# Two score banks as one PSUM tile or as two, the maxima taken apart by head, and another order of the program

## The chip, the core and the metric

The kernel runs on one core of a Trainium2 chip. The metric is device time in microseconds (us). TensorE is called PE below, VectorE DVE, ScalarE ACT, GpSimd POOL; SP issues the DMAs.

## The reference

Attention over 4 batches and 8 heads (576 positions, head size 64, keys masked by blocks of 64), and behind it two MLP layers on the 2304 rows of width 512:

```python
scores = scale * np.matmul(q, k.transpose(0, 1, 3, 2))
scores = np.where(block_i >= block_j, scores, -1000000000.0)
scores = scores - np.max(scores, axis=-1, keepdims=True)
attn = np.exp(scores)
attn = attn / (np.sum(attn, axis=-1, keepdims=True) + 1e-09)
x = np.matmul(attn, v)                     # rows: batch, position; columns: head, 64
...
h = x @ w_in                               # layer 1: 512 to 2048
g = h * np.tanh(np.where(h > 20.0, h, np.log1p(np.exp(np.minimum(h, 20.0)))))
x = g @ w_out                              # 2048 to 512
...
h = np.maximum(x @ w_in2, 0.0)             # layer 2
out = h * h @ w_out2
```

The MLP weights come as float64. The kernel decodes them to fp32 on DVE and ACT.

## The kernel before

**Chunks and passes.** The rows are cut into six chunks of 384 (`CH1`). Chunks 0 and 1 hold the first 192 positions of the batches (`attention_lo`, in fp32), chunks 2 to 5 the other 384 positions of one batch each (`attention_hi`, 4 head pairs a chunk, so 16 pairs). Each chunk goes through both MLP layers, a pass for each, in the order of `PASSES`. A pass is 16 steps of 128 hidden columns: 12 matmuls into `hp` (L1209), the activation `h` on ACT (L1215), the split of g into two fp16 halves (L1034 on ACT or L1035 on POOL, then L745 on DVE), and 12 matmuls into the four accumulators `acc` (L1275). Products are made of three fp16 products, of high and low halves. These are the bulk of PE's work. The pass of chunk 0 in layer 1 is done in fp32 (L1229, L1244) while the weights are still being split (`decode`, `weigh`, `split`).

**A head pair in `attention_hi`.** A small matmul with a matrix of ones gives the scale of q and k over the partitions (L808, read by DVE at L811), another that of v (L760, L762). The scores of both heads go to two PSUM banks, head 0 to bank 0 and head 1 to bank 1 (L833; the mask is L836). DVE takes the maxima of both heads in one reduction (`peak`, L843). In the first of the three score tiles of a pair it also copies 128 further columns of each head out (L889), the tail of the third tile. `low` scales the maxima (L846), ACT takes exp with a running sum, once for each head (`expo`, L851). `finish` normalizes and splits (L870 on ACT, L745 on DVE) and issues the transposing DMA (L874). Four head pairs later the product with v follows (L931), into bank 0, and ACT takes it out (L944).

**The two banks.** Both are one PSUM tile, `spare`, [128, 2, 512]. Columns 0 to 447 of each bank hold scores, the product with v, or a work tile of `attention_lo`. The last 64 columns of bank 0 hold the small sums: of q and k (`qm`), of v (`vm`), of the weights (`sc`, L1081, read by DVE at L1087) and of a chunk's maxima (`sx`, L1151, read at L1153). The other six banks are the four `acc` and the two `hp`.

**What sets the order.** Every step is a task with an engine, its reads and its writes. A planner (`Sched`) once put them in order with assumed durations; the result is stored as a string (`PLAN`), which `planned` decodes: the place of each task, and its engine where there is a choice. Each engine runs its part of this list strictly in order. The planner keeps engines off a bank by `opened`: PE waits for the last ACT or DVE access of the bank, ACT and DVE for the last of PE. The waits in the program itself are put in by the tile framework, from the accesses in the order of the list. `norm` adds the squares of a chunk on ACT (L1168) and DVE (L1171, L1172) and sums them on PE into `hp` (L1173).

Of the kernel before, what the change touches and what calls it, by code (L numbers as in the profile page):

```python
# [58 lines left out]
def seg_len(tiles):  # L59
# [35 lines left out]
    "RbG<*e9F+nSge_OR{Eg95a}g{kabXd%1P}m$F#rXlWzQeTwayYa<?4T2k_!S-K@i;JF8FXQ0XGiN*S|`+kUIPWPq&I&a#D@|5^UQ`F&-huFw&Z%;&H4Ik{B^"
    "OEX!`{2*y153zbB^QqcYzUHYf_N*;mXdh1d8vA76*A_CARm-%MRFmEMIjfdvN2w~G=}~sx$GvJHd7+kJ-+VOqNcTud`G8fO<wjP$r#H$w`U$$ct#`^oErnec"
    "=uGsP&-0u5KGF2Pu0*R<GFOYrySjoq&Cvn+sm{iJb99l`lf~Lr{z??)GYfUG<dFH2!_3tW**O)z&(l}6i8PS&+T7HW7c?r3&3Ua$)YX(pdaGQ~*Y&hKrN?!O"
    "rV?kb=qvK1p2Jr!==G9Be5Gmwd4?GIiw@J0#Me-r!0N&Jy6lqT=BT#OW^%pMVyv{;gO_&d24eew?vRINootgXx=p_$vQzW{?$8f!7L@OGl=Rl`i2Qs~PTFc7"
    ">8@M#7H-{He$X%EGi-d9b|Al&={jt`o_M;Q+oefCcC5v^Dda^LS*5w9slF*+YBOyl(}-px%e5Xm*UJ=HV4g$ACHjPXsMWNFwwB5A3bqw(&iinpuAE%P4~_6_"
    "C!+2jW+h(ei&w|W*YcLO<Fwaxo=!F&=~9`?$?tI99QJi2R_1798Dk!n8Js`bOw$?qju~YV_}ou=%XD383dvhiMFyKFJ9lB@J~G9O*YdJeCV&H*Ipq%NDql!h"  # L100
    "8AD{3#O`;=Nba1f<IDw_NE|$+BZ<Gf@|YRRX|36pQ$}ll{SRW|oU|~liLjAG)<n~s7#yKprH%~3Ly6K*?v%Goec7y!^8O%rGQ#xIfqEPGG#pFZB)!P+szg?2"
    "Jpd9kl?pNo1Zgbg&3#$~e|04KnqYxHYhSYaHqC1qf_4d<&`ArM=d_d7W^XT|sJ-Sfjr6kSk`6@KFL?D<ZKdVpJ!z%4W8+HP@DlU4Ni(vcJh50p8tcRQ2B_DF"
# [1496 lines left out]
```

## Time and profile before

| | before |
|---|---|
| median of 3 runs | 942.67 us (934.58 to 943.70) |
| profiled execution | 941.45 us, span 939.4 us |
| PE busy | 901.2 us, 96% of the span |
| ACT busy | 618.9 us, 66% |
| DVE busy | 574.7 us, 61% |
| mean granted clock of PE | 0.994 |

The span runs from the first to the last instruction of the profiled execution. A busy time is the time in which at least one instruction of the engine's datapath runs. The names in the rows are those of the program, without buffer numbers; `spare` is the tile of the two score banks, `pad` holds the results of exp, `late` and `pt` the transposed ones. A share over the span mixes stages, so the stretches matter more than the shares.

### The profile page before, as it was taken

What the parts mean: (1) busy time and instruction counts of PE and PEld (TensorE: products, weight loads), DVE (VectorE), ACT (ScalarE), POOL (GpSimd) and SP (SyncE); (2) the same over time, 40 slices, a digit from 0 to 9 for tenths busy, and PEclk for the clock granted to TensorE, in tenths of its full rate; (3) what the DMA queues carried; (4) which work ended last, traced back from release to release, by engine and by line L of the source; (5) the groups of instructions that cost most, each with busy time, mean ns of one, the idle gap of its engine ahead of it and who ended that gap; (6) DMA issues with size and microseconds to landing.
All of it is one profiled execution on the core that took longest, in us unless ns stands there. A gap on an engine that the chain in (4) does not pass through costs nothing. (4 is left out here: it accounts for less than half of the span.)

```text
span 939.4 us, 15711 instructions
## 1 busy us (share of the span) xinstructions
PE 901.2 (96%) x5786; PEld 532.3 (57%) x5786; DVE 574.7 (61%) x1386; ACT 618.9 (66%) x1177; POOL 82.5 (9%) x114
## 2 busy tenths in 40 slices
PE   7989997999999999999999999999999999999997
PEld 6655553555555555555556555555566666666664
DVE  6969998999989854455871486777441251331211
ACT  7979998998798875475892586676642242444442
POOL 0000101220110100011110011121100000000000
PEclk9999998999999999999999999999999999999999
DMA  9866576799668687786773378688832222333530
GB/s 350 293 223 235 206 184 191 183 289 290 245 216 234 199 226 228 193 169 229 195 153 99 113 204 226 164 201 178 199 102 68 68 68 68 112 135 135 168 112 34
DMA packets 141772, 168.79 MB, mean 180 GB/s; under 512 B 105856, under 2 KB 110976, under 8 KB 137600
## 3 DMA queue, kind: packets, MB, share of 16 engines
q1 hardware_dynamic: 141696, 167.80, 60.6%
q8 instruction: 45, 0.74, 0.3%
q14 instruction: 31, 0.25, 0.1%
HBM read 125.30 MB, written 17.30 MB: 152 GB/s over the span
## 5 line engine op out<-in xcount | busy, mean ns | idle before, releaser
L745 DVE SCALAR_TENSOR_TENSOR g<-h,cst,g 128x384 f16<-128x384 f32 x176 | 108.0, 617 | 233.5 <-ACT g L1034 222.7
L1215 ACT ACTIVATE h<-hp,cst 128x384 f32<-128x384 f32 x176 | 101.1, 577 | 216.4 <-PE hp L1209 211.1
L1275 PE MATMUL acc<-g,ws 128*128 128x384 f16 x1128 | 229.7, 326 | 2.7 <-DMA ws<-wspill 1.6
L1275 PE MATMUL acc<-g,raw 128*128 128x384 f16 x984 | 204.6, 326 | 0.0
L1209 PE MATMUL hp<-x,first 128*128 128x384 f16 x768 | 157.8, 330 | 3.8 <-ACT h L1215 3.8
L1275 PEld LDWEIGHTS <-ws 128*128 128x128 f16 x1128 | 108.7, 98 | 78.1 <-issue 5.4
L1209 PEld LDWEIGHTS <-first 128*128 128x128 f16 x960 | 92.7, 99 | 70.7 <-issue 13.0
L1275 PEld LDWEIGHTS <-raw 128*128 128x128 f16 x984 | 95.5, 98 | 63.0 <-issue 0.6
L1209 PE MATMUL hp<-x,raw 128*128 128x384 f16 x552 | 117.9, 326 | 0.0
L1209 PE MATMUL hp<-x,ws 128*128 128x384 f16 x408 | 85.0, 328 | 0.0
L1209 PEld LDWEIGHTS <-raw 128*128 128x128 f16 x648 | 61.6, 98 | 41.1 <-issue 2.0
L745 DVE SCALAR_TENSOR_TENSOR pb<-pad,st,pb 128x384 f16<-128x384 f32 (+2 forms) x96 | 72.0, 756 | 20.2 <-ACT pb L870 20.1
L1034 ACT ACTIVATE g<-h,cst 128x384 f16<-128x384 f32 x123 | 75.1, 612 | 13.3 <-PE acc L1275 12.5
L870 ACT ACTIVATE pb<-pad,st 128x384 f16<-128x384 f32 (+2 forms) x96 | 66.7, 711 | 15.0 <-DVE st L863 4.9
L851 ACT ACTIVATE pad<-spare,st,sq 128x448 f32<-128x448 f32 (+1 forms) x96 | 65.2, 680 | 15.8 <-DVE st L846 9.2
L1035 POOL TENSOR_SCALAR g<-h,cst 128x384 f16<-128x384 f32 x53 | 43.1, 815 | 342.5 <-PE acc L1275 129.7
L1209 PEld LDWEIGHTS <-ws 128*128 128x128 f16 x504 | 48.5, 98 | 32.3 <-issue 1.8
L843 DVE TENSOR_REDUCE st<-spare 128x2 f32<-128x896 f32 (+1 forms) x48 | 47.8, 996 | 11.4 <-PE spare L836 9.5
L1229 PE MATMUL hp<-xs,first 128*128 128x384 f32 x128 | 49.5, 495 | 0.1
L1220 ACT ACTIVATE h<-h 128x384 f32<-128x384 f32 x85 | 43.5, 513 | 0.8
L1209 PE MATMUL hp<-late,first 128*128 128x384 f16 x192 | 41.7, 326 | 0.0
L833 PE MATMUL spare<-q 64*128 64x448 f16 (+2 forms) x384 | 39.0, 309 | 2.7 <-ACT pad L851 1.6
(229 smaller groups left out, 1152.0 us busy)
## 6 DMA issues: line engine op xcount, KB each, us to landing
ws<-wspill SPq DMA_DIRECT2D x68, 512.0 KB, 4.4
...
```

The source lines that it names most:

```text
L745: return sch.add("DVE", c_dve(n) + 62 * ap, lambda: nc.vector.scalar_tensor_tensor(dst(), a(), s() if ap else s, c(), op0, op1), r=r, w=w, ...
L833: nc.tensor.matmul(out=pp.t[:, hd, o:o + k1 - k0], lhsT=qh.t[rows, u, a:a + 128], rhs=qh.t[rows, w, nq + k0:nq + k1], start=p == 0, stop=p ...
L843: sch.add("DVE", c_dve(2 * (o1 - o0)), lambda: nc.vector.reduce_max(both(st, j, r0), pp.t[r0:, :, o0:o1], axis=AX.X), w=[(pp, 0), (st, j)])
L851: t = sch.add("ACT", c_act(o1 - o0, True, 3), lambda hd=hd: nc.scalar.activation(pf[hd].t[r0:, k0:k0 + o1 - o0], pp.t[r0:, hd, o0:o1], AF. ...
L870: sch.add("ACT", c_act(n, False, 1), lambda pb=pb, pv=pv, s=s: nc.scalar.activation(pb.t[:, 0:i + 1, 0, :], pv(), AF.Copy, scale=s()), r=[ ...
L1034: "ACT": ("ACT", c_act(n, False, 1), lambda: nc.scalar.activation(dst(0), src(), AF.Copy, scale=s()), False),
L1035: "POOL": ("POOL", c_pool(n, False), lambda: nc.gpsimd.tensor_scalar(dst(0), src(), s(), 1.0, ALU.mult, ALU.mult), False),
L1209: nc.tensor.matmul(out=hp.t[:, 0:n], lhsT=w.t[:, f % 2, a, 128 * k:128 * k + 128], rhs=x.t[:, c, k, 0:n], start=k == 0 and i == 0, stop=k ...
L1215: sch.add("ACT", c_act(n, True, 1), lambda: nc.scalar.activation(h.t[:, 0:n], hp.t[:, 0:n], (AF.Mish, AF.Relu)[l], scale=hs()), r=[(cst, ( ...
L1220: "ACT": ("ACT", c_act(n), lambda: nc.scalar.activation(hv(), hv(), AF.Square), False),
L1229: nc.tensor.matmul(out=hp.t[:, 0:n], lhsT=wf.t[:, 512 * (f % 2) + 128 * k:512 * (f % 2) + 128 * k + 128], rhs=xs.t[:, k, 0:n], start=k == ...
L1275: nc.tensor.matmul(out=acc.t[:, 0:n], lhsT=wo.t[:, f % 2, a, 128 * m:128 * m + 128], rhs=g.t[:, c, 0:n], start=f == 0 and i == 0, stop=f = ...
```

## The change

The tile `spare` becomes two tiles of one bank each, `bank[0]` and `bank[1]`. The small sums move from bank 0 to the last 64 columns of bank 1. `peak` takes the maximum of each head by an instruction of its own, and the copy of the tail is two copies. The scores are declared by head, so that the exp of a head depends on its own bank; for the planner the product with v holds bank 0 alone, and `opened` now sets each of PE, ACT and DVE against both others. `PLAN` is another string of the same kind; it has 64 tasks more. Lines behind `low` stand 4 to 9 further down: L843 is L845, L851 is L856, L889 is L895, L1087 is L1096, L1172 is L1181, L1173 is L1182, L1209 is L1218, L1215 is L1224.

```diff
@@ -88,86 +88,87 @@
 PLAN = (
-    "c-p<13B1kay2qb)tz{l#i%q7=nDLlpR^&)U#xkXZGA5-==_t)nk{nVrA*ri_>f{iTkeSGAV{i7(W@Bggzt8>t|L=coyYBtmQ}>>8?bh1=^$ySbywC7^e$QS-"
...
+    "c-p<13B1ka_W#$j_ddo9A@dZ;JiBC`k|~sw5HgiAg=B~%6(Jdlx=K=plDhRvG)S7v5gCtpJjZxAhhzFa>;L{vn_K_a?{<Gv+y0)tpJ6@gS;J?2);UE)^;Rh<"
...
 )
@@ -278,7 +279,7 @@
 
     def opened(self, t, name):
 
-        others = ("ACT", "DVE") if name == "PE" else ("PE",)
+        others = [o for o in ("PE", "ACT", "DVE") if o != name]
         return max((self.shut[b, o] + self.SEM[o][name] for b in t.banks for o in others if (b, o) in self.shut), default=0.0)
 
     def fill(self, now, start, t):
@@ -681,13 +682,13 @@
     hps = [psp.tile([128, 512], F32, tag=f"hp{i}", name=f"hp{i}") for i in range(2)]
     R["hp"] = fixed(hps)
 
-    spare = {"ab": psp.tile([128, 2, 512], F32, tag="pab", name="spare")}
-    R["sc"] = fixed([spare["ab"][:, 0, 448 + 4 * i:452 + 4 * i] for i in range(4)])
-    R["qm"] = fixed([spare["ab"][:, 0, 464:472], spare["ab"][:, 0, 472:480]])
-    R["sx"] = fixed([spare["ab"][:, 0, 496:504], spare["ab"][:, 0, 504:512]])
-    R["vm"] = fixed([spare["ab"][:, 0, 480:488], spare["ab"][:, 0, 488:496]])
-    R["s1"] = fixed([spare["ab"][:, 1, 0:448], spare["ab"][:, 0, 0:448]])
-    R["ab"] = fixed([spare["ab"][:, :, 0:448]])
+    bank = [psp.tile([128, 512], F32, tag=f"bank{i}", name=f"bank{i}") for i in range(2)]
+    R["sc"] = fixed([bank[1][:, 448 + 4 * i:452 + 4 * i] for i in range(4)])
+    R["qm"] = fixed([bank[1][:, 464:472], bank[1][:, 472:480]])
+    R["sx"] = fixed([bank[1][:, 496:504], bank[1][:, 504:512]])
+    R["vm"] = fixed([bank[1][:, 480:488], bank[1][:, 488:496]])
+    R["s1"] = fixed([bank[1][:, 0:448], bank[0][:, 0:448]])
+    R["ab"] = fixed([[t[:, 0:448] for t in bank]])
     for key, extra in EXTRAP.items():
         R[key].bufs += extra
 
@@ -830,27 +831,31 @@
                 for p, (u, w) in enumerate(((0, 0), (1, 0), (0, 1))):
                     for hd in range(2):
                         rows = slice(64 * hd, 64 * hd + 64)
-                        nc.tensor.matmul(out=pp.t[:, hd, o:o + k1 - k0], lhsT=qh.t[rows, u, a:a + 128], rhs=qh.t[rows, w, nq + k0:nq + k1],
+                        nc.tensor.matmul(out=pp.t[hd][:, o:o + k1 - k0], lhsT=qh.t[rows, u, a:a + 128], rhs=qh.t[rows, w, nq + k0:nq + k1],
                                          start=p == 0, stop=p == 2 and not mask)
                 for hd in range(2 if mask else 0):
-                    nc.tensor.matmul(out=pp.t[:, hd, o + k1 - k0 - 64:o + k1 - k0], lhsT=above, rhs=never[:, 0:1].to_broadcast([128, 64]), start=False, stop=True)
-
-            steps.append(sch.add("PE", 3 * (c_mm16(k1 - k0) + 16) + (110.0 if mask else 0.0), mm, r=[(qh, (p, j)) for p in range(2) for j in range(2)], w=[(pp, 0)]))
+                    nc.tensor.matmul(out=pp.t[hd][:, o + k1 - k0 - 64:o + k1 - k0], lhsT=above, rhs=never[:, 0:1].to_broadcast([128, 64]), start=False, stop=True)
+
+            steps.append(sch.add("PE", 3 * (c_mm16(k1 - k0) + 16) + (110.0 if mask else 0.0), mm, r=[(qh, (p, j)) for p in range(2) for j in range(2)], w=[(pp, 0), (pp, 1)]))
 
         both = lambda st, j, r0=0: st.t[r0:, 2 * j:2 * j + 2]
 
-        def peak(st, j, pp, r0, o0, o1):
-            sch.add("DVE", c_dve(2 * (o1 - o0)), lambda: nc.vector.reduce_max(both(st, j, r0), pp.t[r0:, :, o0:o1], axis=AX.X), w=[(pp, 0), (st, j)])
-
-        def low(st):
+        def peak(st, j, pp, o0, o1):
+            for hd in range(2):
+                t = sch.add("DVE", c_dve(o1 - o0), lambda hd=hd: nc.vector.reduce_max(st.t[:, 2 * j + hd:2 * j + hd + 1], pp.t[hd][:, o0:o1], axis=AX.X),
+                            w=[(pp, hd), (st, (j, hd))])
+                t.banks = (hd,)
+
+        def low(st, r):
             sch.add("DVE", 69.0, lambda: nc.vector.tensor_scalar(both(st, 2), both(st, 0), sq.t[:, 5:6], None, ALU.mult),
-                    r=[(st, 0), (sq, 5)], w=[(st, 2)], lat=70.0)
+                    r=[(sq, 5), *r], w=[(st, 2)], lat=70.0)
 
         def expo(st, j, pp, r0, o0, o1, pf, k0):
+            view = lambda hd: pp.t[hd] if j == 4 else pp.t[:, hd]
             for hd in range(2):
                 t = sch.add("ACT", c_act(o1 - o0, True, 3), lambda hd=hd: nc.scalar.activation(
-                    pf[hd].t[r0:, k0:k0 + o1 - o0], pp.t[r0:, hd, o0:o1], AF.Exp, bias=st.t[r0:, 4 + hd:5 + hd], scale=sq.t[r0:, 4:5],
-                    accum_out=st.t[r0:, 2 * j + hd:2 * j + hd + 1]), r=[(st, 2), (sq, 4)], w=[(pp, 0), (st, (j, hd)), (pf[hd], k0)], table="exp")
+                    pf[hd].t[r0:, k0:k0 + o1 - o0], view(hd)[r0:, o0:o1], AF.Exp, bias=st.t[r0:, 4 + hd:5 + hd], scale=sq.t[r0:, 4:5],
+                    accum_out=st.t[r0:, 2 * j + hd:2 * j + hd + 1]), r=[(st, 2), (sq, 4)], w=[(pp, hd), (st, (j, hd)), (pf[hd], k0)], table="exp")
                 t.banks = (hd,) if j == 4 else ()
 
         def merge(st, j, op, r, w):
@@ -88,86 +88,87 @@
 PLAN = (
-    "c-p<13B1kay2qb)tz{l#i%q7=nDLlpR^&)U#xkXZGA5-==_t)nk{nVrA*ri_>f{iTkeSGAV{i7(W@Bggzt8>t|L=coyYBtmQ}>>8?bh1=^$ySbywC7^e$QS-"
...
+    "c-p<13B1ka_W#$j_ddo9A@dZ;JiBC`k|~sw5HgiAg=B~%6(Jdlx=K=plDhRvG)S7v5gCtpJjZxAhhzFa>;L{vn_K_a?{<Gv+y0)tpJ6@gS;J?2);UE)^;Rh<"
...
 )
@@ -911,12 +918,14 @@
                     qa = max(q0, 128 * c) - q0
                     for j, i in ((0, 0), (1, 0), (0, 1)):
                         for hd in range(2):
-                            streams[hd].append((ptv(hd)[:, 2 * c + i, qa:nq], av.t[64 * hd:64 * hd + 64, 0, qa:nq], part(j, c, hd)))
+                            streams[hd].append((ptv(hd)[:, 2 * c + i, qa:nq], av.t[0][64 * hd:64 * hd + 64, qa:nq], part(j, c, hd)))
                 products(streams)
 
             step = sch.add("PE", sum(3 * c_pair(nq - max(q0, 128 * c) + q0) for c in range(nch)) + 98, mm_av, r=[v3, *pts], w=[av])
             step.rows = 0.86
-            settle(lambda: av.t[:, 0, 0:nq], av, nq, x, hp, xo, sv)
+            settle(lambda: av.t[0][:, 0:nq], av, nq, x, hp, xo, sv)
+            for t in av.tasks:
+                t.banks = (0,)
             return [step]
 
         return steps, second
@@ -1493,12 +1502,12 @@
         for inst in R[key].insts:
             for t in inst.tasks:
                 if t.eng in ("PE", "ACT", "DVE") and t.banks is None:
-                    t.banks = (0, 1) if key == "ab" else (1 - inst.idx % 2,) if key == "s1" else (0,)
+                    t.banks = (0, 1) if key == "ab" else (1 - inst.idx % 2,) if key == "s1" else (1,)
...
```

The new order at three places. DVE, before, at the first score tile of head pair 2 in chunk 2: `st` are the maxima, `tl` the tail, `sq` the scale of the next pair, `nsq` the squares of a chunk, `wst` the sums of weights, `cst` and `x` the constants and halves of a chunk.

```order
L843 TENSOR_REDUCE st_1312<-spare 128x2
L1171 TENSOR_TENSOR nsq_1294<-nsq_1294,wsq_1307 128x768
L846 TENSOR_SCALAR st_1312<-st_1312,sq_1085 128x2
L745 SCALAR_TENSOR_TENSOR x_73<-xs_1149,cst_1215,x_73 128x384
L889 COPY tl_1327<-spare 128x256
```

And with the change:

```order
L1201 TENSOR_TENSOR cst_909<-cst_909 128x1
L746 SCALAR_TENSOR_TENSOR vs<-vs,sv_976 128x640
L845 TENSOR_REDUCE st_1318<-bank_133 128x1
L812 TENSOR_SCALAR sq_1286<-bank_134 128x2
L845 TENSOR_REDUCE st_1318<-bank_134 128x1
L813 TENSOR_SCALAR sq_1286<-sq_1286 128x2
L895 COPY tl_1333<-bank_133 128x128
L746 SCALAR_TENSOR_TENSOR x_73<-xs_1147,cst_1270,x_73 128x384
```

Each maximum and each tail copy is two instructions, with the scale of the next pair (L812, L813) between them.

DVE right behind that, before, to the step of the norm that PE's L1173 needs:

```order
L1195 TENSOR_TENSOR cst_893<-cst_893,wst_638 128x1
L811 TENSOR_SCALAR sq_1274<-spare 128x2
L745 SCALAR_TENSOR_TENSOR wn_66<-late,us_838,wn_66 128x1024
L745 SCALAR_TENSOR_TENSOR x_73<-xs_1149,cst_1215,x_73 128x384
L812 TENSOR_SCALAR sq_1274<-sq_1274 128x2
L1196 TENSOR_SCALAR cst_893<-cst_893 128x1
L1087 TENSOR_SCALAR wst_1071<-spare 128x2
L1172 TENSOR_TENSOR nsq_1294<-nsq_1294 128x384
L1029 TENSOR_SCALAR cst_893<-cst_893 128x1
```

With the change:

```order
L1204 TENSOR_TENSOR cst_909<-cst_909,wst_777 128x1
L814 TENSOR_SCALAR sq_1286<-sq_1286 128x2
L1180 TENSOR_TENSOR nsq_1326<-nsq_1326,wsq_1316 128x768
L1205 TENSOR_SCALAR cst_909<-cst_909 128x1
L895 COPY tl_1333<-bank_134 128x128
L1038 TENSOR_SCALAR cst_909<-cst_909 128x1
L850 TENSOR_SCALAR st_1318<-st_1318,sq_1041 128x2
L746 SCALAR_TENSOR_TENSOR wn_66<-late,us_829,wn_66 128x1024
L1181 TENSOR_TENSOR nsq_1326<-nsq_1326 128x384
L746 SCALAR_TENSOR_TENSOR pb<-pad,st_1128,pb 128x4x128
L746 SCALAR_TENSOR_TENSOR first<-first,us_453 128x1024
L1207 TENSOR_SCALAR cst_909<-wst_777,cst_909 128x16
```

The read of the weights' sum (L1087, now L1096) stood ahead of the norm's step L1172, now L1181; it has gone 24 rows behind it. A step of `finish` (`pb`) has come behind it instead.

ACT in chunk 2, later, at two exp groups of the next head pair: `h` is the activation of a pass, `ACT_TABLE_LOAD` the change between its table and that of exp.

```order
L851 ACT_TABLE_LOAD
L851 ACTIVATE pad,st_1753<-spare,st_1753,sq_1274 128x448
L870 ACTIVATE pb<-pad,st_1632 128x3x128
L851 ACTIVATE pad,st_1753<-spare,st_1753,sq_1274 128x448
L1215 ACT_TABLE_LOAD
L1215 ACTIVATE h_1811<-hp_131,cst_893 128x384
L1060 ACTIVATE wf<-raw_68 128x1024
L1078 ACTIVATE wsq_1848,us_1849<-wf 128x1024
L870 ACTIVATE pb<-pad,st_1632 128x3x128
L851 ACT_TABLE_LOAD
L851 ACTIVATE pad,st_1673<-tl_1651,st_1673,sq_1274 128x128
L851 ACTIVATE pad,st_1673<-spare,st_1673,sq_1274 128x448
```

With the change:

```order
L856 ACT_TABLE_LOAD
L856 ACTIVATE pad,st_1758<-bank_133,st_1758,sq_1286 128x448
L856 ACTIVATE pad,st_1758<-bank_134,st_1758,sq_1286 128x448
L1069 ACTIVATE wf<-raw_68 128x1024
L875 ACTIVATE pb<-pad,st_1625 128x3x128
L1087 ACTIVATE wsq_1846,us_1847<-wf 128x1024
L1043 ACTIVATE g_1858<-h_1782,cst_909 128x384
L875 ACTIVATE pb<-pad,st_1758 128x4x128
L1043 ACTIVATE g_1871<-h_1799,cst_909 128x384
L856 ACTIVATE pad,st_1745<-bank_133,st_1745,sq_1286 128x448
L856 ACTIVATE pad,st_1745<-tl_1639,st_1745,sq_1286 128x128
L856 ACTIVATE pad,st_1745<-bank_134,st_1745,sq_1286 128x448
```

The two exp of a tile follow each other, and the loads for one activation between this group and the next are gone.

## Rows read from the trace of the kernel before

**Rows 1.** The page: span; engine, busy us, share of the span, instructions.

```profile
span 939.4 us, 15711 instructions
...
PE 901.2 (96%) x5786; PEld 532.3 (57%) x5786; DVE 574.7 (61%) x1386; ACT 618.9 (66%) x1177; POOL 82.5 (9%) x114
```

**Rows 2.** Stretches: length, busy us (instructions) by engine, granted clock, DMA share, GB/s.

```profile
0.00:75.00 75.00, 64.73 (x336) 44.64 (x337) 58.79 (x160) 60.27 (x164) 1.05 (x10) 1.00 0.81 294
75.00:150.00 75.00, 72.99 (x322) 39.87 (x321) 73.46 (x177) 72.36 (x123) 7.33 (x10) 1.00 0.62 200
150.00:164.00 14.00, 9.47 (x51) 4.20 (x51) 10.15 (x31) 10.93 (x18) 1.70 (x3) 0.76 0.62 174
164.00:250.00 86.00, 79.24 (x565) 46.08 (x564) 83.32 (x175) 77.43 (x121) 13.67 (x15) 1.00 0.83 245
250.00:350.00 100.00, 94.91 (x628) 54.71 (x627) 80.61 (x202) 82.88 (x143) 12.78 (x16) 0.98 0.74 226
350.00:700.00 350.00, 345.47 (x2448) 201.85 (x2447) 208.81 (x523) 224.86 (x451) 41.99 (x54) 1.00 0.69 178
700.00:900.00 200.00, 200.00 (x1235) 120.41 (x1233) 52.74 (x114) 76.89 (x141) 4.00 (x6) 1.00 0.31 105
900.00:940.00 40.00, 34.43 (x212) 20.53 (x210) 6.80 (x11) 13.25 (x26) 0.00 (x0) 0.97 0.18 59
```

**Rows 3.** Waits of PE, 75 to 350: us, times, longest us.

```profile
PE hp L1209 <- ACT h L1215: 3.8, 4, 1.4
PE hp L1173 <- DVE cst L1029: 3.1, 1, 3.1
PE spare L1081 <- ACT pad L851: 1.8, 2, 1.0
PE acc L1275 <- DMA ws<-wspill: 1.6, 1, 1.6
PE spare L833 <- ACT pad L851: 1.6, 3, 1.0
```

**Rows 4.** Timeline of PE: start, us, line, operation, tiles, count, idle time before.

```profile
159.49 0.48 PE L1173 MATMUL hp<-nsq,ones 128*128 128x384 bf16 x1 [3.15 <-DVE cst L1029]
159.76 2.12 PE L1209 MATMUL hp<-x,first 128*128 128x384 f16 x6
...
163.03 1.14 PE L1209 MATMUL hp<-x,first 128*128 128x384 f16 x6
```

**Rows 5.** Timeline of DVE, around 159 us.

```profile
153.42 0.42 DVE L889 COPY tl<-spare 128x256 f32<-128x256 f32 x1
153.75 0.15 DVE L1195 TENSOR_TENSOR cst<-cst,wst 128x1 f32<-128x1 f32 x1
...
159.01 0.16 DVE L1087 TENSOR_SCALAR wst<-spare 128x2 uint32<-128x2 uint32 x1 [3.18 <-ACT pad L851]
159.09 0.35 DVE L1172 TENSOR_TENSOR nsq<-nsq 128x384 bf16<-128x384 bf16 x1
...
163.23 1.09 DVE L843 TENSOR_REDUCE st<-spare 128x2 f32<-128x896 f32 x1 [0.67 <-PE spare L836]
164.24 0.61 DVE L745 SCALAR_TENSOR_TENSOR g<-h,cst,g 128x384 f16<-128x384 f32 x1
```

**Rows 6.** Timeline of ACT, around 157 us.

```profile
156.97 1.28 ACT L851 ACT_TABLE_LOAD   x1
158.27 0.62 ACT L851 ACTIVATE pad<-spare,st,sq 128x320 f32<-128x320 f32 x1
```

**Rows 7.** Waits of DVE, 75 to 350, for exp.

```profile
DVE wst L1087 <- ACT pad L851: 9.9, 6, 3.2
```

**Rows 8.** Groups by line and shape: count, busy us, mean ns, idle before.

```profile
L843 DVE TENSOR_REDUCE st<-spare 128x2 f32<-128x896 f32 x32 | 34.7, 1084 | 5.9 <-PE spare L836 4.2 <-PE spare L833 1.8
...
L889 DVE COPY tl<-spare 128x256 f32<-128x256 f32 x16 | 6.6, 412 | 0.2 <-PE spare L1081 0.2
```

**Rows 9.** Stretch 75 to 350, DVE of line L843, then of L889.

```profile
75.00:350.00 275.00, 23.33 (x28) 0.98 0.73 222
...
75.00:350.00 275.00, 2.86 (x7) 0.98 0.73 222
```

**Rows 10.** Groups by line on ACT: table loads ahead of exp.

```profile
L851 ACT ACT_TABLE_LOAD x20 | 25.7, 1283 | 1.1 <-DVE us L1029 0.4 <-DVE cst L1183 0.3
```

More of the change, by code (lines that the diff above doesn't have):

```diff
@@ L95 @@
[L95 to L102, printed above, removed]
@@ L171 @@
+    "ga9pm@c8ORLv;3C7)<yf6q+g|?IEUzOfDz^5feJk1o!d`8$f3m-l27Ua^|}u78a$zkU@R~Mhrc8Q}P;#lfz)mjglRUGYAu}wh~g)pgshoGe`{yT9KO*%mj5W"
+    "q^dzj5%q~uG$^kgc1A<;8@s`QeHVM<0Z$Z(lb%@M{8-32V*!4|0&ED2ML_@m?6jyKF<#{{aRL|#1Ioj_ID-iqo#1NGfM^C~HAI*YD&y@#9Lr3cdc}ff<wm4L"
+    "ZUk4{Pf@?;xslB=Kfj`W5(b$haTtmC^fc<76rynGwy;JARUv5ALaF~_nD9R`92hNR7$Jn*yw3#4>)*nJ6-DB#E$SN~8n7b?b2}23E;lzyCXoGqc*}nQpW*$2"
+    "w$uylKi$xCwYhP{kSfLge91^)+nYe>FY5AtH4~4{_^b~ZvHyKd{y!7{@^jpo0sVG=Hxm1Q4mJu*"
 )
@@ L886, in attention_hi @@
                 steps.append(halves(vs, v3, sv, R["vm"].new()))
-            peak(st, 0, pp, 0, 0, n)
+            peak(st, 0, pp, 0, n)
             if i == 2:
-                sch.add("DVE", c_dve(256), lambda pp=pp, n=n: nc.vector.tensor_copy(tail.t, pp.t[:, :, n:n + 128]), w=[(pp, 0), tail])
-                peak(last, 1, tail, 0, 0, 128)
-            low(st)
+                for hd in range(2):
+                    t = sch.add("DVE", c_dve(128), lambda pp=pp, n=n, hd=hd: nc.vector.tensor_copy(tail.t[:, hd], pp.t[hd][:, n:n + 128]), w=[(pp, hd), (tail, hd)])
+                    t.banks = (hd,)
+                sch.add("DVE", c_dve(256), lambda: nc.vector.reduce_max(both(last, 1), tail.t, axis=AX.X), r=[(tail, 0), (tail, 1)], w=[(last, 1)])
+            low(st, [(st, (0, 0)), (st, (0, 1))])
             expo(st, 4, pp, 0, 0, n, pf, 0)
@@ L895, in attention_hi @@
         scores(4, pp, 0, 0, 448, False)
-        peak(last, 0, pp, 0, 0, 448)
-        merge(last, 0, ALU.max, [(last, 1)], [(last, 0)])
-        low(last)
+        peak(last, 0, pp, 0, 448)
+        merge(last, 0, ALU.max, [(last, 1), (last, (0, 0)), (last, (0, 1))], [(last, 0)])
+        low(last, [(last, 0)])
         expo(last, 5, tail, 0, 0, 128, pf, 448)
@@ L1500, in tile_attention_moe @@
             for _ in range(t.fillers or 0):
-                nc.tensor.matmul(out=spare["ab"][:, 1, 448:512], lhsT=ones, rhs=ones[:, 0:64], start=True, stop=True)
+                nc.tensor.matmul(out=bank[1][:, 448:480], lhsT=ones, rhs=ones[:, 0:32], start=True, stop=True)
             t.fn()
```

147 lines of the change are left out of this document (76 added, 71 removed).

## The prediction

> **What bounds the kernel now.** I read the page first: the span is 939.4 us and TensorE (PE) is busy in 901.2 of it [rows 1]. The change adds and removes no matmul, so all it can return or cost is PE's 38.2 us of idle time, and what PE loses at the lower clock. The view by stretches says where that is [rows 2]: 10.3 us before 75 us, 18.4 us from 75 to 350 us (2.0 + 4.5 + 6.8 + 5.1), 4.5 us from 350 to 700, nothing from 700 to 900, and 5.6 us at the tail, where the last output is written. The first two attention chunks, up to some 90 us, keep their order but for swaps of neighbours, and the tail is untouched. So the question is the 18.4 us from 75 to 350 us. There DVE is busy in 73.46 of 75 us, then in 83.32 of 86, and ACT in 72.36 of 75 and 77.43 of 86: PE is the bound, but two engines behind it have no slack, and what delays them reaches PE. After 350 us DVE is busy for 208.81 of 350 us, and small delays there are covered.
>
> The waits of PE in that stretch are many and small [rows 3]: 3.8 us for h (ACT's activation), 3.1 for one norm, 1.8 and 1.6 for an exp on the score banks, 1.6 for a DMA. The longest one shows a mechanism. The timeline of PE has the norm's matmul L1173 at 159.49, 3.15 us late [rows 4]. DVE stood idle for 3.18 us before L1087, the read of a small sum (two columns of bank 0), and the norm's own step L1172 is queued right behind it [rows 5]. L1087 waited for ACT's exp of head 0 on other columns of the same bank, which began only at 158.27, after a table load of 1.28 us [rows 6]; it ended at 158.89 and DVE went on at 159.01. So readers of one bank exclude each other here, though neither writes it, and the planner of before knew nothing of that (its rule for a bank sets ACT and DVE against PE alone). The cluster around it, 150 to 164 us, is dear: 4.5 us of PE idle, and a granted clock of 0.76 [rows 2]. That mean is 6.7 us at 1.2 GHz and the rest at 2.4, or some 3.4 us of work lost: six matmuls of L1209 take 2.12 us at 159.76 and 1.14 us at 163.03 [rows 4].
>
> **The change, part by part.** *Two tiles for one.* No instruction moves by that; which waits exist is settled by bank, as it was.
>
> *Maxima and tail copy by head.* 48 reductions become 96 and 16 copies 32: 64 more DVE instructions, with as many elements in all. The price of one is the fixed part. One bound is the duration: 1084 ns for 896 columns and 412 ns for 256 [rows 8] are 1.05 ns a column and 143 ns fixed. The other is the spacing of starts on a busy DVE: L889 to the next 0.33 us, L843 (896) to the next 1.01 us [rows 5], which is 1.06 ns a column and about 60 ns fixed, since an instruction starts before the last one's row ends. I take 66 ns, because it is throughput that counts when DVE is full: 64 x 0.066 = 4.2 us in all (upper bound 9.2). By 350 us L843 has run 28 times and the copy L889 7 times [rows 9]; 7 of the 28 are reductions of the copied tail, which stay whole, so 21 + 7 = 28 are taken apart: 28 x 0.066 = 1.8 us (upper bound 4.0). The other 2.4 us lie after 350 us, under DVE's idle time.
> The Trainium skill ("Perfetto Trace Analysis", Optimizing Scalar/DVE Operations) speaks against this part: about 125 ns of busy time for each DVE instruction on PSUM, and larger operations where the engine is saturated. By that figure the 28 would cost an estimated 3.5 us; the spacing of starts here shows about half.
>
> *Small sums to bank 1, and the new order.* DVE lost 9.9 us in six waits of L1087 for the exp [rows 7], all from 75 to 350 us. Counted over the whole order, a DVE access stands directly behind an ACT access of the same bank 10 times before and 4 times now. At the same share, 6/10 of 9.9 us, 5.9 us of DVE come back against 1.8 us spent. The sums are also clear of the product with v now, which stays in bank 0; no row shows a wait that this ends, so it counts nothing. At the cluster the sum's read has gone from the place ahead of the norm's step to 24 rows behind it. What remains there: from the start of head 0's maximum to the end of L1181 (L1172 before), DVE has 15 instructions, which at the spacings above and the durations of their rows make some 4.3 us; PE has 12 matmuls there, about 2.0 us, and the small ones. PE still waits about 2.2 us in place of 4.5: 2.3 us returned (bounds 0 and 4.5). With half the idle time one of the two falls of the clock may go: half of 3.4, 1.7 us (bounds 0 and 3.4).
>
> *Table loads and movements of work.* ACT has 44 table loads instead of 48, all four gone before some 210 us: 4 x 1.283 = 5.1 us [rows 10]. Against it, ACT takes over 12 more of POOL's g steps than it gives, and gives nearly as much other work to POOL and DVE: about 1 us more for ACT. The rest falls where ACT has been 90 to 96% busy. PE's waits for exp and h are 3.8 + 1.8 + 1.6 us [rows 3]; I give a fifth of the 5.1 us, 1.0 us, to PE (bounds 0 and 5.1).
>
> *PE's and SP's orders.* PE's bulk matmuls keep their sequence but for shifts of a few steps, the single steps of attention move by mostly under ten, and one by 78, the scale of a head pair in chunk 3. Of SP's 376 DMA steps 76 change places, none by more than 14; no transfer is added. The longest of PE's waits for a DMA in the stretch is 1.6 us [rows 3]. A new order can make waits as well as remove them. I take 0 with bounds of -5 and +5 us, the size of what the single stretches hold now [rows 2].
>
> **The sum**, against the profiled execution's own 941.45 us (span 939.4 and 2.0 around it): -2.3 - 1.7 - 1.0 = -5.0, with the 1.8 us of DVE paid from the 5.9. That gives 936.5; I say 937. The median of the runs is 942.67, 1.2 us above the profiled one, and one run was 934.58, so the kernel has executions that are as short as my forecast.
>
> **Rivals.**
> *The whole middle is repaired.* If the new order, made with a rule that knows of readers excluding each other, takes away both falls of the clock at the cluster (3.4) and half of the 18.4 us, 12.6 us go: 929. For it: three of the five waits [rows 3] are on the score banks or, as the norm's, behind them. Against it: DVE and ACT are still nearly full there, and 4 of 10 direct successions remain. Chance 0.20.
>
> *It does nothing.* The banks were apart already where it counts, one wait removed is another found: 941, with -2 and +3. For it: PE is 96% busy, and of its 18.4 us idle only one wait is longer than 1.6 us; the rest is spread as in any order. And a read still excludes a read: what L1087 met in bank 0 [rows 5, 6], head 0's exp, it meets in bank 1 as head 1's. The Trainium skill ("PSUM — Partial Sum Buffer", PSUM bank collisions raise a hardware error) says the same of any two engines on one bank, so that by it two tiles free nothing that the order does not free; the trace agrees, with the 3.18 us. Chance 0.20.
>
> *DVE pays.* The stalls do not come back, and the upper price of the split, 28 x 0.143 = 4.0 us, goes one for one to PE in a stretch where DVE is 97% busy: 945.5. For it: DVE's share [rows 2]. Against: the spacing of starts. Chance 0.08.
>
> *Bank 1 is crowded (slower).* All 63 small sums (L808, L760, L1081, L1151) are now in the bank that head 1's exp reads last, where they were in the one that head 0's leaves first. PE is in order: a small sum that waits holds all bulk matmuls behind it. One such wait is 0.9 us now (1.8 in two, [rows 3]). It decides from about 11 of the 63: 11 x 0.9 = 9.9 us, 951; with one more fall of the clock (1.7) 953. Against it: before, ACT followed by PE in the sums' bank 62 times, now 53 times, and only a few of them cost anything. Chance 0.09.
>
> **How the numbers follow.** The forecast has 0.43 (933 to 940), the whole repair 0.20 (926 to 933), nothing 0.20 (939 to 944), DVE 0.08 (944 to 947), the crowd 0.09 (949 to 956). The range of 929 to 947 takes in the forecast, the two that change little, DVE's price and half of the repair; it leaves out the crowd and the better half of the repair. About 1% is what a measurement of this kernel can tell from no change: faster is below 933.2, slower above 952.1, from the median. Nearly all of the repair lies below 933.2: 0.20. Of the crowd most is above 952: 0.08. The rest, 0.72, is no change.
>
> **What would show it.** Right: no idle row of 3 us before the norm's matmul near 155 us, and a granted clock above 0.85 there; DVE's waits of L1096 for exp below 5 us in total; DVE's busy time higher by 4 us by starts, up to 9 by rows; ACT with 44 table loads; PE idle of 12 to 15 us from 75 to 350 us; PE's busy time shorter by the clock alone. The split maxima should read near 0.61 us for 448 columns. Wrong: PE waiting on bank tiles for more than the 1.8 + 1.6 us of now, L1090 and L762 first; a new fall of the clock elsewhere; a DMA wait of over 2 us from the new order of SP.

## The result and the profile after

The changed kernel takes 927.89 us in the median, against 940.32 for the kernel before in the same comparison: a ratio of 0.985, 95% interval 0.9815 to 0.9886 (the quotient of the two medians is 0.987). The median counts an execution that was disturbed (2369.74 us), which the ratio leaves out; the others took 924.07 to 928.33 us, 927.45 in the median. The forecast was 937 us with a range of 929 to 947. The time lies just below the range, and between the profiled executions 14.0 us were gained where 5.0 were forecast.

The profiled execution took 927.45 us. The page, with the line of span and engines that answers to [rows 1]:

```profile
span 925.7 us, 15738 instructions
...
PE 895.3 (97%) x5786; PEld 531.3 (57%) x5786; DVE 580.7 (63%) x1453; ACT 615.1 (66%) x1174; POOL 74.1 (8%) x110
```

The span is 13.7 us shorter. PE's idle time went from 38.2 to 30.4 us, which is 7.8. PE's busy time is 5.9 us shorter with the same 5786 matmuls. Some 3.4 us of that is the clock: it fell to half for 3.4 us at a time, three times in mid-run before and once now, and the bulk matmuls of L1209, now L1218, on `first` (768 in each kernel) went from a mean of 330 to 326 ns. What the other 2.5 us are is not shown. The view by stretches, columns as in [rows 2]:

```profile
0.00:75.00 75.00, 69.00 (x352) 48.79 (x353) 64.84 (x176) 63.57 (x168) 1.36 (x11) 0.98 0.86 313
75.00:150.00 75.00, 71.43 (x343) 39.37 (x342) 73.82 (x195) 72.44 (x126) 7.25 (x10) 1.00 0.56 179
150.00:164.00 14.00, 11.15 (x72) 5.78 (x72) 14.00 (x35) 13.94 (x24) 4.27 (x6) 1.00 1.13 270
164.00:250.00 86.00, 80.46 (x574) 46.67 (x572) 82.79 (x176) 78.02 (x126) 8.52 (x10) 1.00 0.92 264
250.00:350.00 100.00, 96.04 (x640) 55.93 (x638) 80.43 (x205) 80.03 (x141) 11.14 (x17) 1.00 0.77 229
350.00:700.00 350.00, 346.57 (x2456) 202.13 (x2455) 207.75 (x551) 221.03 (x439) 37.55 (x51) 1.00 0.67 172
```

Against [rows 2], PE gets through more matmuls in each of these stretches (its busy time is shorter in one, 71.43 for 72.99 us), but the first one stands out: 4.3 us more in the first 75 us (69.00 for 64.73), where I had expected nothing. The stretch of the cluster, 150 to 164 us, is at full clock now (1.00 for 0.76). Matched by the count of bulk matmuls done, the changed kernel is 3.8 us ahead at 62 us, 9.1 at 190, 12.7 at 266, 14.3 at 436 and 13.8 from about 600 us to the end.

What the first stretch lost before is in rows that I had not weighed. PE's waits from 50 to 75 us in the kernel before (us, times, longest):

```profile
PE spare L967 <- ACT pt L977: 1.7, 1, 1.7
PE spare L1081 <- ACT pt L977: 0.6, 1, 0.6
PE spare L967 <- DVE xs L723: 0.5, 1, 0.5
PE spare L967 <- ACT xs L721: 0.4, 1, 0.4
PE spare L1005 <- DVE pt L723: 0.3, 1, 0.3
```

In the changed kernel that view is empty. The timeline of before there (start, us, engine and line, tiles, idle time before) shows two units of `attention_lo` on `spare`, the first in bank 1, the next in bank 0 (the pool `s1` alternates between them):

```profile
55.15 0.42 ACT L977 ACTIVATE pt<-spare,st 128x192 f32<-128x192 f32 x1
...
55.71 1.08 PE L967 MATMUL spare<-qk 128*128 128x192 f32 x6 [1.72 <-ACT pt L977]
...
56.96 0.56 DVE L972 TENSOR_REDUCE st<-spare 128x2 f32<-128x384 f32 x1 [1.62 <-PE spare L968]
...
57.55 0.42 ACT L977 ACTIVATE pt<-spare,st 128x192 f32<-128x192 f32 x1 [1.89 <-DVE st L972]
...
58.10 0.22 DVE L973 TENSOR_REDUCE st<-spare 128x1 f32<-128x64 f32 x1 [0.58 <-ACT pt L977]
58.35 0.31 ACT L977 ACTIVATE pt<-spare,st 128x64 f32<-128x64 f32 x1 [0.29 <-DVE st L973]
```

The three exp of ACT belong to the first unit, whose maxima were ready at 53.6 us. PE's scores and DVE's two reductions belong to the next unit, in the other bank. Only one of the waits is needed: DVE needs the scores that PE has just written. The others are between units that share no data, yet they go one at a time: PE waits for the first exp, the second exp for DVE's first reduction, DVE's second reduction for that exp, and the third exp for DVE's second reduction. The changed kernel at the same work, ACT alone:

```profile
54.19 0.42 ACT L986 ACTIVATE pt<-bank,st 128x192 f32<-128x192 f32 x1
54.50 0.19 ACT L986 ACTIVATION_READ_ACCUMULATOR pt<-bank,st 128x1 f32 x1
54.80 0.42 ACT L986 ACTIVATE pt<-bank,st 128x192 f32<-128x192 f32 x1
...
55.21 0.41 ACT L986 ACTIVATE pt<-bank,st 128x192 f32<-128x192 f32 x1
...
55.61 0.42 ACT L986 ACTIVATE pt<-bank,st 128x192 f32<-128x192 f32 x1
```

The exp follow each other without a wait.

Of the wait that the prediction was built on [rows 4, 5], this is what remains in the timeline of PE after the change:

```profile
148.71 0.32 PE L1182 MATMUL hp<-nsq,ones 128*128 128x384 bf16 x1 [2.09 <-DVE nsq L1181]
148.87 1.14 PE L1218 MATMUL hp<-x,first 128*128 128x384 f16 x6
```

The norm's matmul waits 2.09 us where it waited 3.15, and the six matmuls behind it take 1.14 us where they took 2.12. DVE's wait of the weights' sum for exp, 9.9 us in [rows 7], is not in the changed kernel's list at all. The maxima, and ACT's table loads ahead of exp, by group:

```profile
L856 ACT ACT_TABLE_LOAD x18 | 23.1, 1283 | 0.5 <-DVE st L850 0.2
...
L845 DVE TENSOR_REDUCE st<-bank 128x1 f32<-128x448 f32 x64 | 37.4, 616 | 9.7 <-PE bank L837 5.4 <-PE bank L834 4.3
...
L845 DVE TENSOR_REDUCE st<-bank 128x1 f32<-128x320 f32 x32 | 14.7, 482 | 6.3 <-PE bank L837 6.0
```

616 ns for 448 columns is as forecast, and so are ACT's table loads: 44 in all for 48, of which 18 for 20 [rows 10] are ahead of exp. DVE's busy time is 6.0 us higher (580.7 for 574.7).

### The profile page after: what moved, and what is told of

It is laid out like the page before. It is cut to its first block, busy times and chain, and to the rows that moved or that the text cites. A ratio compares the mean times of both kernels' runs of the same rounds, so it can differ in the third digit from the quotient of the medians.

```text
span 925.7 us, 15738 instructions
## 1 busy us (share of the span) xinstructions
PE 895.3 (97%) x5786; PEld 531.3 (57%) x5786; DVE 580.7 (63%) x1453; ACT 615.1 (66%) x1174; POOL 74.1 (8%) x110
## 5 line engine op out<-in xcount | busy, mean ns | idle before, releaser
L746 DVE SCALAR_TENSOR_TENSOR g<-h,cst,g 128x384 f16<-128x384 f32 x176 | 110.8, 632 | 233.7 <-ACT g L1043 216.5
L1224 ACT ACTIVATE h<-hp,cst 128x384 f32<-128x384 f32 x176 | 101.1, 578 | 222.2 <-PE hp L1218 207.7
L1218 PE MATMUL hp<-x,first 128*128 128x384 f16 x768 | 155.0, 326 | 4.1 <-ACT h L1224 3.6
L1218 PEld LDWEIGHTS <-first 128*128 128x128 f16 x960 | 92.1, 98 | 69.2 <-issue 10.4
L1218 PE MATMUL hp<-x,raw 128*128 128x384 f16 x552 | 117.7, 326 | 0.0
L1043 ACT ACTIVATE g<-h,cst 128x384 f16<-128x384 f32 x135 | 82.4, 613 | 21.1 <-PE acc L1284 18.0
L1218 PE MATMUL hp<-x,ws 128*128 128x384 f16 x408 | 84.8, 326 | 0.7 <-DMA ws<-wspill 0.7
L1218 PEld LDWEIGHTS <-raw 128*128 128x128 f16 x648 | 61.7, 98 | 40.2 <-issue 1.1
L746 DVE SCALAR_TENSOR_TENSOR pb<-pad,st,pb 128x512 f16<-128x512 f32 (+2 forms) x96 | 71.5, 753 | 13.0 <-ACT pb L875 12.7
L856 ACT ACTIVATE pad<-bank,st,sq 128x448 f32<-128x448 f32 (+1 forms) x96 | 65.0, 679 | 7.1 <-DVE st L850 5.2
L1218 PEld LDWEIGHTS <-ws 128*128 128x128 f16 x504 | 48.0, 98 | 33.5 <-DMA ws<-wspill 1.8
L845 DVE TENSOR_REDUCE st<-bank 128x1 f32<-128x448 f32 (+1 forms) x96 | 52.1, 571 | 16.0 <-PE bank L837 11.4
L1238 PE MATMUL hp<-xs,first 128*128 128x384 f32 x128 | 47.5, 491 | 0.0
L1044 POOL TENSOR_SCALAR g<-h,cst 128x384 f16<-128x384 f32 x41 | 28.7, 702 | 190.7 <-PE acc L1284 76.7
L834 PE MATMUL bank<-q 64*128 64x448 f16 (+2 forms) x384 | 39.7, 306 | 3.2 <-ACT xs L953 2.7
L1218 PE MATMUL hp<-late,first 128*128 128x384 f16 x192 | 41.7, 326 | 0.0
```

What stands on the lines that cost most here:

```text
L746: return sch.add("DVE", c_dve(n) + 62 * ap, lambda: nc.vector.scalar_tensor_tensor(dst(), a(), s() if ap else s, c(), op0, op1), r=r, w=w, ...
L834: nc.tensor.matmul(out=pp.t[hd][:, o:o + k1 - k0], lhsT=qh.t[rows, u, a:a + 128], rhs=qh.t[rows, w, nq + k0:nq + k1], start=p == 0, stop=p ...
L845: t = sch.add("DVE", c_dve(o1 - o0), lambda hd=hd: nc.vector.reduce_max(st.t[:, 2 * j + hd:2 * j + hd + 1], pp.t[hd][:, o0:o1], axis=AX.X) ...
L856: t = sch.add("ACT", c_act(o1 - o0, True, 3), lambda hd=hd: nc.scalar.activation(pf[hd].t[r0:, k0:k0 + o1 - o0], view(hd)[r0:, o0:o1], AF. ...
L1043: "ACT": ("ACT", c_act(n, False, 1), lambda: nc.scalar.activation(dst(0), src(), AF.Copy, scale=s()), False),
L1044: "POOL": ("POOL", c_pool(n, False), lambda: nc.gpsimd.tensor_scalar(dst(0), src(), s(), 1.0, ALU.mult, ALU.mult), False),
```

## The experiments

Three things came with the change: another order, two tiles, and maxima apart with the sums in bank 1. The first runs take the order and the code apart. Theory A is the prediction's: the order did it. Theory B: the code did it.

**The changed code in the old order.**

```diff
 # the changed kernel
 PLAN = (
-    "c-p<13B1ka_W#$j_ddo9A@dZ;JiBC`k|~sw5HgiAg=B~%6(Jdlx=K=plDhRvG)S7v5gCtpJjZxAhhzFa>;L{vn_K_a?{<Gv+y0)tpJ6@gS;J?2);UE)^;Rh<"
...
+    "c-p<13Ea))*8Z=1?~Q~qMo5yO0g)*~h9ps>LdFaw9Vb(rN}{7d%G-$~iUuhurCB<4(x6gFipWfv9`iheeXsZXn;z<aKL68sC%^W7_P&R8uX_#Gy4LfQl35X*tvV{Gqjr"
...
```

> The changed code (two tiles, small sums in bank 1, maxima and tail copy by head) in the order and with the engines of the kernel before; the two halves of a maximum or a copy stand next to each other. Theory A, the new order brings the gain: 938 to 945 us, the three falls of the clock and the waits at 50 to 75 and 150 to 164 us are all there. Theory B, the banks bring it (sums out of the bank that the product with v and head 0 use): 926 to 932 us.

928.44 us, ratio 0.9854 (0.9824 to 0.9885): the whole gain, without the new order.

**The old code in the new order.**

```diff
 # the kernel before; each pair of halves is one instruction again
 PLAN = (
-    "c-p<13B1kay2qb)tz{l#i%q7=nDLlpR^&)U#xkXZGA5-==_t)nk{nVrA*ri_>f{iTkeSGAV{i7(W@Bggzt8>t|L=coyYBtmQ}>>8?bh1=^$ySbywC7^e$QS-"
...
+    "c-p<13A~Qw*8kUaKaXJ>GmjxEnJJN3C{szs5K#!Bgc1oSsZL6vkV+{^rP4XlagvmIn`NGd%{FCYn>P2g{@;6gIQ9ShPv`x=@7rxZ`+2TmUF%xIZ~fM@b3`?dl#x3nhg{"
...
```

> The code before (one tile, small sums in bank 0, one reduction for both heads, one tail copy) in the order and with the engines of the change; a merged instruction stands where the later of the two stood. Theory A: 925 to 931 us. Theory B: 937 to 944 us. If the sums in bank 0 now stand behind head 0's exp or behind the product with v at places the new order did not provide for, 932 to 937.

941.04 us, ratio 0.9997 (0.9977 to 1.0016): nothing. Theory A falls.

**The order by halves.** Both kernels are the changed code; only `PLAN` differs: the first 501 tasks, up to the first score of `attention_hi` at some 95 us, in the old order and the rest in the new, and the other way round.

> The changed code and the new order, but with the first 500 tasks (to the first score of attention_hi, some 95 us) in the old order. If the first 95 us bring the 4 us that the traces show there on their own: 931 to 933 us. If the early part only moves waits that come anyway later: 927 to 929 us.

929.67 us, ratio 0.9864 (0.9836 to 0.9893), between the two ranges.

> The changed code, the first 500 tasks in the new order and all others in the old one. If early and late part add up: 935 to 938 us, with the falls of the clock near 152 and 159 us still there. If the early part alone brings most: 928 to 931 us. If it does nothing without the rest: 939 to 943 us.

930.14 us, ratio 0.9875 (0.9842 to 0.9908). All four orders of the changed code lie within 2.3 us of each other, and their intervals overlap. What is left is the code, in three parts: the tiles (theory C), the maxima by head (D), the sums' bank (E).

**The maxima alone.** One tile, sums in bank 0, old order; `peak` and the copy of the tail as in the change.

```diff
 # the kernel before
-        def peak(st, j, pp, r0, o0, o1):
-            sch.add("DVE", c_dve(2 * (o1 - o0)), lambda: nc.vector.reduce_max(both(st, j, r0), pp.t[r0:, :, o0:o1], axis=AX.X), w=[(pp, 0), (st, j)])
+        def peak(st, j, pp, o0, o1):
+            for hd in range(2):
+                t = sch.add("DVE", c_dve(o1 - o0), lambda hd=hd: nc.vector.reduce_max(st.t[:, 2 * j + hd:2 * j + hd + 1], pp.t[hd][:, o0:o1], axis=AX.X),
...
```

> One tile, small sums in bank 0, order and engines of before; only the maxima and the tail copies are taken apart by head. Theory C (the framework sets its waits by tile, so that one tile holds both banks for every access, and two tiles are what helps): 940 to 944 us, the price of 64 DVE instructions. Theory D (the maxima by head are what helps, since a bank comes free earlier): 926 to 934 us.

941.44 us, ratio 0.9994 (0.9968 to 1.0019). The split neither costs nor brings anything that can be measured. D falls.

**One tile again**, all else as in the changed code in the old order; every access keeps its bank and columns.

```diff
 # the changed code in the old order
-    bank = [psp.tile([128, 512], F32, tag=f"bank{i}", name=f"bank{i}") for i in range(2)]
+    spare = psp.tile([128, 2, 512], F32, tag="pab", name="spare")
+    bank = [spare[:, 0], spare[:, 1]]
```

> x1_new_code_old_order with both banks as views of one tile: maxima and copies by head, small sums in bank 1, old order. Theory C: 939 to 944 us, like the kernel before. Theory E (the bank of the small sums is what helps): 927 to 932 us.

942.72 us, ratio 1.0021 (0.9996 to 1.0045): with this edit alone the whole gain is gone. The stretches of these two kernels, the changed code in the old order with two tiles:

```profile
0.00:75.00 75.00, 68.38 (x352) 47.65 (x353) 63.34 (x172) 63.67 (x173) 1.05 (x10) 1.00 0.86 314
75.00:350.00 275.00, 259.75 (x1636) 147.96 (x1635) 247.88 (x604) 247.22 (x410) 35.18 (x45) 1.00 0.76 227
```

And with one:

```profile
0.00:75.00 75.00, 64.83 (x336) 44.87 (x337) 58.77 (x160) 60.11 (x163) 1.05 (x10) 1.00 0.81 293
75.00:350.00 275.00, 255.60 (x1571) 144.32 (x1570) 250.15 (x610) 245.15 (x404) 36.53 (x44) 0.99 0.75 223
```

One tile gives the numbers of before (64.73 in [rows 2]) and PE's old waits: in the list of that kernel `spare` L972 waits 1.7 us for ACT's `pt` L982, as L967 did. In the programs one can count the waits: of DVE's accesses of the score banks 21 wait for ACT before and with one tile, 8 with two. The instructions, banks and order are the same, so the 13 further waits come from the tile, which the framework guards as one thing, reads against reads included. DVE's read of the weights' sum, in bank 1 in both kernels, shows this on its own. Its waits for exp with two tiles:

```profile
DVE wst L1091 <- ACT pad L851: 1.0, 1, 1.0
```

And with one:

```profile
DVE wst L1092 <- ACT pad L852: 7.5, 6, 1.9
```

Five of the six with one tile, 6.9 us, are for an exp that reads bank 0: a read of one bank waits for a read of the other.

**The sums back in bank 0**, two tiles, old order.

```diff
 # the changed code in the old order
-    R["sc"] = fixed([bank[1][:, 448 + 4 * i:452 + 4 * i] for i in range(4)])
+    R["sc"] = fixed([bank[0][:, 448 + 4 * i:452 + 4 * i] for i in range(4)])
...
```

> x1_new_code_old_order with the small sums in bank 0: two tiles, maxima and copies by head, old order. Theory C: 927 to 934 us; a few us over x1 (928.4) where a sum's read now stands behind head 0's exp or the product with v. Theory E: 937 to 943 us.

932.34 us, ratio 0.9914 (0.9882 to 0.9946). DVE's wait of the weights' sum (L1091 here) for exp, 1.0 us with the sums in bank 1, is back at 6.9 of its 9.9:

```profile
DVE wst L1091 <- ACT pad L851: 6.9, 5, 1.9
```

This lies where C put it. E, as the whole cause, falls; but some 4 us seemed to hang on the sums' bank, with intervals that just overlap (0.9885 and 0.9882).

**The same thing elsewhere.** If the tile sets the waits, then the two `hp` buffers of the MLP, put into one tile, must be bound to each other too.

```diff
 # the changed kernel
-    hps = [psp.tile([128, 512], F32, tag=f"hp{i}", name=f"hp{i}") for i in range(2)]
+    hpt = psp.tile([128, 2, 512], F32, tag="hp", name="hp")
+    hps = [hpt[:, i] for i in range(2)]
```

> The changed kernel with the two buffers hp (another pair of banks, written by PE by turns and read by ACT) as views of one tile. Theory C: PE then waits at each of the 190 or so steps whose hp matmuls follow those of the step before by less than ACT's h takes (0.58 us and the hand-overs): 935 to 960 us. If waits go by bank and something else is at work in the score banks: 926 to 930 us, no change.

983.48 us, ratio 1.0452 (1.041 to 1.0495), more than I had put. PE's wait of the bulk matmuls for the activation, in that kernel's list:

```profile
PE hp L1219 <- ACT h L1225: 38.4, 113, 2.8
```

In the changed kernel it is 3.6 us in 6 waits. That makes 34.8 of the 56 us; PE's busy time is also 20.3 us longer (915.6 for 895.3), with the same matmuls, which these waits do not explain.

**One tile in the new order.** The edit of the one tile, made to the changed kernel itself.

> The changed kernel, its order and all, with both banks as views of one PSUM tile. Theory C (waits are set by tile, and the two tiles are the whole gain): 939 to 945, within 0.3% of the kernel before; PE busy in the first 75 us 64 to 66, as in the other one-tile kernels (64.73, 64.83, 65.20), where two tiles gave 68.4 to 69.0. Rival A2 (the new order pays too, but only with the maxima taken apart by head, which the run of the new order alone did not have): 930 to 936.

941.43 us, ratio 0.9994 (0.9977 to 1.0011). Theory C holds in the new order too: with this edit alone the whole gain is gone again.

**The sums' bank in the new order**, two tiles; the edit of the sums, made to the changed kernel.

> The changed kernel, its order and all, with the small sums in bank 0 instead of bank 1; two tiles stay. Theory F (with two tiles the sums' bank is worth some 4 us, as in the old order, 932.3 against 928.4): 930 to 934, and DVE's wait of the read of the weights' sum for exp back at 5 us or more. Rival G (the 4 us belong to the old order, where the read stands next to the exp of head 0; the new order has moved it away): 926 to 930, and that wait at 2 us or less.

936.21 us, ratio 0.9946 (0.993 to 0.9962). Neither theory had this much: moving the sums costs 8 us here, more than in the old order, and not by the wait that I had named (2.4 us). The stretches show that the gain has two places. With one tile:

```profile
0.00:75.00 75.00, 65.26 (x336) 44.98 (x337) 59.81 (x163) 58.73 (x155) 1.05 (x10) 1.00 0.81 289
75.00:350.00 275.00, 251.44 (x1541) 142.69 (x1540) 246.79 (x599) 241.93 (x405) 27.82 (x39) 0.99 0.76 224
```

With two tiles and the sums in bank 0:

```profile
0.00:75.00 75.00, 69.76 (x354) 48.55 (x355) 65.22 (x176) 64.12 (x169) 1.79 (x11) 1.00 0.89 316
75.00:350.00 275.00, 253.00 (x1565) 143.29 (x1564) 245.72 (x597) 239.77 (x396) 29.63 (x41) 0.99 0.77 222
```

And the changed kernel, from 75 us on:

```profile
75.00:350.00 275.00, 259.08 (x1623) 147.75 (x1622) 251.04 (x608) 244.43 (x413) 31.18 (x43) 1.00 0.78 228
```

Two tiles alone bring the first 75 us (65.26 to 69.76), `attention_lo`. After that two tiles alone add little (251.44 to 253.00); most comes when the sums leave bank 0 as well (253.00 to 259.08). Bank 0 holds two other things: the scores that head 0's exp reads, and the product with v. The last two runs tell these apart.

**Sums in bank 0, product in bank 1.**

```diff
 # the kernel with the sums in bank 0, new order
-                            streams[hd].append((ptv(hd)[:, 2 * c + i, qa:nq], av.t[0][64 * hd:64 * hd + 64, qa:nq], part(j, c, hd)))
+                            streams[hd].append((ptv(hd)[:, 2 * c + i, qa:nq], av.t[1][64 * hd:64 * hd + 64, qa:nq], part(j, c, hd)))
...
-            settle(lambda: av.t[0][:, 0:nq], av, nq, x, hp, xo, sv)
+            settle(lambda: av.t[1][:, 0:nq], av, nq, x, hp, xo, sv)
```

> The changed kernel, its order and all, with the two tiles' roles changed over: small sums in bank 0, product with v in bank 1. Against 927.9 with sums in bank 1 and product in bank 0, and 936.2 with both in bank 0. Theory P (what counts is that the small sums and the product with v are in different tiles, so that neither waits for the other's read): 927 to 931, PE's waits of the product for the sum's read and of the sums for the product's copy gone. Theory H (what counts is that the sums are off bank 0, which head 0's exp reads): 934 to 938, and the 1.7 us wait of v's sum for exp is still there.

933.91 us, ratio 0.9921 (0.9901 to 0.9941), 0.1 us below the range of theory H and 2.9 above that of theory P.

**Both in bank 1**: the same edit, made to the changed kernel.

> The changed kernel, its order and all, with both the small sums and the product with v in bank 1. Theory P: 934 to 938, the waits between product and sums back (1.6 and 1.3 us among them). Theory H: 927 to 931.

930.32 us, ratio 0.9882 (0.9859 to 0.9906). Theory H holds the larger share. With the product in bank 0 the sums' bank is worth 8.3 us (936.2 to 927.9), with the product in bank 1 it is 3.6 (933.9 to 930.3, with intervals that just overlap). What the product's bank is worth, 2.3 and 2.4 us, lies inside the intervals. PE's waits from 75 to 350 us say the same. With the sums in bank 0 and the product in bank 1:

```profile
PE bank L761 <- ACT pad L856: 1.7, 1, 1.7
...
PE bank L809 <- DVE st L845: 1.2, 1, 1.2
...
PE bank L1090 <- ACT pad L856: 1.1, 1, 1.1
```

These three, small sums of bank 0 that wait for an exp or a maximum, stand in the list of each of the two kernels with the sums in bank 0, and not in the two with the sums in bank 1. With both in bank 1 these stand there:

```profile
PE bank L1090 <- ACT xs L953: 1.3, 1, 1.3
...
PE bank L940 <- DVE wst L1096: 0.5, 1, 0.5
```

They are the sum that waits for the product's copy and the product that waits for the sum's read; both stand in the list with both in bank 0 (1.3 and 1.6), neither in that of the changed kernel.

## Why the prediction was wrong

**The step that failed** is "Two tiles for one. No instruction moves by that; which waits exist is settled by bank, as it was." I costed the edit at nothing. It is the condition of the whole gain: with one tile 941.43 in the new order and 942.72 in the old, with two 927.89 and 928.44. The wait that I had read as two readers of one bank [rows 5, 6] fits a guard on the bank and a guard on the tile alike, since a tile of two banks includes the bank. What would have told them apart was a wait between the two banks, and the trace had it: at 55 to 59 us, and PE's `spare` waits of 50 to 75 us. The rival "It does nothing" expected a sum's read to meet head 1's exp in bank 1 as it had met head 0's in bank 0. In the old order, with two tiles, that wait is 1.0 us, where it was 9.9.

**Where I looked.** "The first two attention chunks, up to some 90 us, keep their order ... So the question is the 18.4 us from 75 to 350 us." That drew the stretch from what the order moved, not from what the edit touched. PE was idle for 10.3 us in the first 75 us, and some 4 of them came back. (The 5.6 us at the tail hold 0.6 us that lie behind the end of the span; nothing hangs on them.)

**The sums in bank 1.** "The sums are also clear of the product with v now ...; no row shows a wait that this ends, so it counts nothing." PE's waits of before held one that could have warned me, L931 (the product) for L811 (the read of a sum), 1.1 us; I did not use it. The product turned out the smaller part. Off the bank of head 0's exp the sums are worth 3.6 to 8.3 us in the three pairs of runs, once the banks are two tiles. The rival "Bank 1 is crowded" has it the other way round: bank 0 was the dearer place.

**The order.** I gave it the stall, the clock and the table loads, 5.0 us in all. Alone it gives 0.9997, and with two tiles 0.985 against 0.9854 without it. Yet it did what I had read from it. PE's longest wait for the norm, 3.1 us in [rows 3], is this in the old code with the new order:

```profile
PE hp L1168 <- DVE nsq L1167: 1.2, 1, 1.2
```

And in the changed kernel with one tile:

```profile
PE hp L1183 <- DVE nsq L1182: 1.3, 1, 1.3
```

Both also have the 44 table loads. Neither is faster than the kernel before (0.9997 and 0.9994), PE's idle time is 41.0 and 40.9 us, against 38.2 [rows 1], and the clock still falls twice in each. So the stall and the loads were real, but with one tile their removal returned nothing that can be measured; I had added them up as if no other wait would take their place. "The whole middle is repaired" (929) had nearly the right time from this wrong source, by luck, and "two tiles free nothing that the order does not free" has it the wrong way round.

**What was right.** PE is the bound, and the gain lies in its idle time and the clock. The stall of the norm fell to 2.09 us, against 2.2 forecast, and the clock there is 1.00 (above 0.85 was forecast). Nothing is gained after 436 us or in the tail. Two signs missed: PE is idle for 15.9 us from 75 to 350 us (12 to 15 forecast), and there is a new fall of the clock, at 18 us. The split of the maxima is nearly free: 64 more instructions and 6.1 us of DVE in the rows of L845 and L895 (52.1 + 8.4 against 47.8 + 6.6), 95 ns each, between the 66 that I took and the upper 143; by the time of the kernel, 0.9994.

**The falls of the clock.** The kernel before has three falls of 3.4 us in mid-run, the changed kernel one (at 18 us, behind a wait of 1.0 us for DVE), the changed code in the old order none. I had counted on one of two at the cluster. Each of these four comes behind idle time of PE, but not every stall brings one: the 2.09 us before the norm's matmul of the changed kernel brought none. The gain does not hang on them alone. The mean granted clock of the executions is 0.998 in the changed kernel and 0.995 in the kernel before, but with the first 501 tasks in the old order it is 0.995 too, at 929.67 us.

**What stays open.** How the 8.3 and the 3.6 us of the sums' bank divide over single waits. Part of the 8.3 may be the clock: of the four kernels compared, the changed one has a mean clock of 0.998 and the other three 0.995, an estimated 3 us of 930. Part may be the order: the code that goes with the new one declares the sums to the planner in bank 1. The old order was made for bank 0 and still gains 3.9 us (932.34 to 928.44). Why bank 1 is the cheaper one is not shown. Nor is whether the chip needs readers of one bank to exclude each other at all; no run tried it.

## What to carry to other kernels

Give each PSUM bank that is used by itself a tile of its own: in a tile of several banks the framework orders the engines against each other across all of it, reads too. When an edit changes how memory is declared, look first at the waits between parts that the new declaration separates, in every stretch where the tile is used, and only then at the order of instructions. Then ask which small accesses share a tile with long ones, and try them in each: here they were cheaper, by 3.6 to 8.3 us, in the bank that head 1's exp reads, though head 0's exp leaves its bank first.

## What had not been expected

The price of one tile differs widely from place to place: the two score banks cost 13 us of 928, the two `hp` buffers, into which half of the bulk matmuls write by turns, 56 us (983.48 for 927.89). That it grows with how often the halves alternate fits these two cases and is not shown by them. A reordering, in which the reductions, the loads of tables and 76 transfers change places, moved the time by less than can be measured, in one tile and in two.
